# Thresholded attention with a gated mix: q's left-over blocks placed by DMA, the sums' 1e-9 on VectorE, low parts in two pieces, and new planned durations

## The chip, the cores and the metric

The kernel runs on one core of a Trainium2 chip. The metric is the device time of one execution in microseconds. Five engines have queues of their own, each worked off in order: TensorE (PE; its weight loads are PEld in the profile), VectorE (DVE), ScalarE (ACT), GpSimd (POOL) and SyncE (SP), which here only issues DMAs.

## What is computed

```python
# attention: q, k, v are (8 batches, 8 heads, 576 rows, 64)
scores = scale * np.matmul(q, k.transpose(0, 1, 3, 2))
thresh = np.max(scores, axis=-1, keepdims=True) - tau
scores = np.where(scores >= thresh, scores, -1000000000.0)
attn = np.exp(scores - np.max(scores, axis=-1, keepdims=True))
attn = attn / (np.sum(attn, axis=-1, keepdims=True) + 1e-09)
x = attn @ v          # heads side by side: (8, 576, 512)
# gated mix
gate = sigmoid(causal convolution of x over 5 rows, per column, with conv_w)
out = (gate * (x @ w_val)) @ w_out
```

The weights `w_val`, `w_out` and `conv_w` arrive as 64-bit floats.

## The kernel before

Two heads of 64 make a pair that fills the 128 partitions. A **job** is one pair of one batch: 32 jobs (4 pairs x 8 batches). The 576 rows of q are four blocks of 128 and a left-over block of 64; the left-over blocks of both heads make one tile together ("both"), so a job has nine tiles: `both`, and four for each head. Arithmetic is float32: for scores and products every operand is split into a high part (rounded to fp32r by ScalarE, `CAST`) and a low part (the difference, `tensor_sub` on GpSimd), and two or three matmuls add up.

For each job `prepare` fetches k and q (`k_r`, `q_r`, one buffer each), scales q on GpSimd (L327), makes `kh`, `kl`, `qh`, `ql` (L312, L316, L320, L324) and copies them by DMA into `KH`, `KL` and `Q`, where every head lies twice over the partitions (L362, L381). The left-over blocks of q go into a block-diagonal operand `bdq`, on GpSimd (`place`, L338 to L349, through `spread`, L210): four instructions of 64x64 for a job. The first job is loaded straight into place on two queues.

For each tile TensorE makes the scores `s` (L482, two buffers), VectorE takes the row maxima (L486), ScalarE the exponentials and the threshold (L492, L494), and VectorE keeps what is over the threshold and sums it (L508). For each group of two tiles (or the single `both` tile), `turned` adds 1e-9 to the sums on GpSimd (L525), takes the reciprocal on VectorE (L527), divides on whichever of GpSimd, ScalarE or VectorE the planner takes (L538, L534, L536), and turns the block with TensorE (L588) and a ScalarE copy (L599). For each half of a job (320 and 256 rows) `attended` multiplies with v (L627, L634). `convolve` makes high and low parts of the result (L667, L671) and the convolution: tap 0 on GpSimd (L676), four taps on VectorE (L683), the gate on ScalarE. When the four pairs of a batch are done, `products` does x @ w_val (L725), the gating on VectorE (L752), high and low parts (L768, L772), and the product with w_out (L725), which ScalarE takes out and SP sends (L797).

The weights are turned from 64-bit words in 16 units of 128x256 (`Words`, `from_f64`): five VectorE steps (L224 to L233), an addition (L236) and a low part (L268) on GpSimd, and two ScalarE steps.

No order is written by hand. Every step is an `op` with an engine, a due number (in tiles), a planned cost, a planned time until its result is there, and the buffers that it takes and gives. `carry_out` (L140) walks planned time: on each engine it takes the earliest that can begin, of equals the one due first, and emits it. GpSimd and those VectorE steps marked `DVEp` also share one planned `port`: no two of them overlap in the plan. The emitted order on every engine is fixed; on the chip each instruction waits by semaphores for what it really needs. A planned duration therefore only decides the order.

## Time and profile before

| | us |
|---|---|
| median of 3 runs | 774.73 |
| lowest, highest | 774.28, 776.41 |
| span of the profiled execution | 776.5 |
| busy PE / DVE / ACT / POOL in it | 719.6 / 644.3 / 647.2 / 475.7 |

The profiled execution's own time is its span, 776.5 us from the first to the last instruction; it is 1.8 us over the median and lies at the upper end of the runs. Busy time is a mean over stages that have different limits, so the views by stretch, by group and along the chain of waits are read beside it. A matmul's end is modelled and overlaps the next one's start.

### The profile page before, as it was taken

How to read it: one execution, taken by the hardware profiler on the slowest of the kernel's cores; microseconds unless marked ns; L12 is line 12 of the kernel's file. 1: busy time of each engine (PE TensorE's matmuls, PEld its weight loads, DVE VectorE, ACT ScalarE, POOL GpSimd, SP SyncE). 2: the span in 40 equal slices, each digit the busy share in tenths (PEclk: the TensorE clock that was granted, in tenths of full speed). 3: DMA queues.
4: the chain of work that ended last, by engine and by line, in shares of the span. 5: the costliest groups of instructions: out<-in, count | busy, mean ns of one | idle time of the engine just before them, and what ended most of it. 6: DMA issues, size and time to landing. Idle time of an engine off the chain costs nothing.

```text
span 776.5 us, 15682 instructions
## 1 busy us (share of the span) xinstructions
PE 719.6 (93%) x5216; PEld 607.0 (78%) x5216; DVE 644.3 (83%) x1359; ACT 647.2 (83%) x1477; POOL 475.7 (61%) x698
## 2 busy tenths in 40 slices
PE   3788778979999999999999999998999999999997
PEld 3556457867878888888888888887888888978897
DVE  5989998988888887999878887887888888899830
ACT  5898978978998889899889988897898989888832
POOL 4777655847676775677557675765556764745321
PEclk9999989999999999999999999999999999999999
DMA  6666553535464555555465565553555556540001
GB/s 183 172 170 153 151 149 86 151 91 151 124 156 118 125 148 146 141 135 138 111 164 118 129 152 142 143 131 79 152 151 123 126 136 163 144 98 26 32 31 62
DMA packets 51888, 99.03 MB, mean 128 GB/s; under 512 B 9056, under 2 KB 9056, under 8 KB 51808
## 3 DMA queue, kind: packets, MB, share of 16 engines
q1 hardware_dynamic: 51488, 97.47, 49.0%
q8 instruction: 42, 0.69, 0.4%
q10 hardware_dynamic: 320, 0.56, 0.3%
q14 instruction: 38, 0.31, 0.1%
HBM read 35.74 MB, written 9.44 MB: 58 GB/s over the span
## 4 chain that ended last, share of the span: by engine, by line
PE 68%; DVE 15%; DMA 5%; POOL 4%; ACT 4%; issue 2%; SPq 0%; POOLq 0%; ACTq 0%
PE acc L725 20%; PE s L482 17%; PE acc L634 14%; PE tp L588 13%; DVE nm L486 4%; DVE pp L508 4%; PE acc L627 3%; DMA q_r<-qT 3%; DVE pre L683 3%; ACT e L492 1%; POOL pp L538 1%; DVE spare L229 1%; DVE spare_m L231 1%; POOL ql L324 1%; DVE pp L536 1%
## 5 line engine op out<-in xcount | busy, mean ns | idle before, releaser
L486 DVE TENSOR_REDUCE nm<-s 128x1 f32<-128x576 f32 x288 | 214.9, 752 | 46.9 <-PE s L482 43.6
L492 ACT ACTIVATE e<-s,nm 128x576 f32<-128x576 f32 x288 | 215.3, 747 | 29.9 <-DVE nm L486 16.3
L508 DVE SCALAR_TENSOR_TENSOR pp<-s,nm,e 128x576 f32<-128x576 f32 x256 | 206.8, 811 | 19.9 <-ACT nm L494 18.3
L599 ACT COPY T<-tp 128x384 f32<-128x384 f32 x384 | 175.2, 488 | 26.3 <-PE tp L588 24.8
L482 PE MATMUL s<-KH,Q 128*128 128x288 f32 x512 | 163.4, 334 | 34.2 <-DVE pp L508 23.1
L588 PE MATMUL tp<-ident,pp 128*128 128x128 f32 x1152 | 183.3, 280 | 10.8 <-ACT pp L534 3.6
L588 PEld LDWEIGHTS tp<-ident,pp 128*128 128x128 f32 x1152 | 141.2, 143 | 20.9 <-ACT T L599 5.2
L482 PE MATMUL s<-KL,Q 128*128 128x288 f32 x512 | 147.0, 301 | 0.0
L482 PEld LDWEIGHTS s<-KH,Q 128*128 128x128 f32 x512 | 99.9, 195 | 59.6 <-DVE pp L508 32.2
L634 PE MATMUL acc<-T,v 128*64 128x256 f32 (+1 forms) x1024 | 141.2, 419 | 0.0
L538 POOL TENSOR_SCALAR pp<-pp,sums 128x576 f32<-128x576 f32 x124 | 106.9, 867 | 36.1 <-DVE sums L527 32.2
L683 DVE SCALAR_TENSOR_TENSOR pre<-xT,cw,pre 128x576 f32<-128x576 f32 x128 | 118.6, 926 | 8.8 <-POOL pre L676 8.7
L634 PEld LDWEIGHTS acc<-T,v 128*64 128x64 f32 x1024 | 69.1, 139 | 64.9 <-issue 28.0
L482 PEld LDWEIGHTS s<-KL,Q 128*128 128x128 f32 x512 | 99.9, 195 | 0.0
L525 POOL TENSOR_SCALAR sums<-sums 128x2 f32<-128x2 f32 (+1 forms) x160 | 46.9, 293 | 82.5 <-DVE pp L508 66.1
L494 ACT ACTIVATE nm<-nm,less 128x1 f32<-128x1 f32 x288 | 84.8, 294 | 0.0
L725 PE MATMUL acc<-xl,wvh 128*128 128x320 f32 (+1 forms) x256 | 78.3, 306 | 1.0 <-POOL xl L671 1.0
L725 PE MATMUL acc<-xh,wvl 128*128 128x320 f32 (+1 forms) x256 | 79.2, 309 | 0.0
L725 PE MATMUL acc<-gl,woh 128*128 128x320 f32 (+1 forms) x256 | 78.2, 305 | 1.1 <-POOL gl L772 1.1
L725 PE MATMUL acc<-xh,wvh 128*128 128x320 f32 (+1 forms) x256 | 78.6, 307 | 0.1
L725 PE MATMUL acc<-gh,wol 128*128 128x320 f32 (+1 forms) x256 | 78.6, 307 | 0.0
L725 PE MATMUL acc<-gh,woh 128*128 128x320 f32 (+1 forms) x256 | 78.4, 306 | 0.0
(81 smaller groups left out, 1279.8 us busy)
## 6 DMA issues: line engine op xcount, KB each, us to landing
KH<-kh SPq DMA_DIRECT2D x124, 144.0 KB, 2.6
KL<-kl SPq DMA_DIRECT2D x124, 144.0 KB, 3.5
k_r<-kT SPq DMA_DIRECT2D x32, 320.0 KB, 3.8
v<-vs SPq DMA_DIRECT2D x32, 320.0 KB, 2.9
q_r<-qT SPq DMA_DIRECT2D x32, 288.0 KB, 3.9
outT<-o SPq DMA_DIRECT2D x32, 288.0 KB, 2.4
Q<-qh SPq DMA_DIRECT2D x62, 128.0 KB, 2.3
Q<-ql SPq DMA_DIRECT2D x62, 128.0 KB, 2.4
```

The source lines that it names most:

```text
L482: nc.tensor.matmul(s[:, a, :HS], w, m, start=i == 0, stop=i == len(terms) - 1)
L486: nc.vector.tensor_reduce(self.nm[:, 0:1], self.s[:, :, :HS], axis=AX.XY, op=ALU.max, negate=True)
L492: nc.scalar.activation(self.e, self.s[:, :, :HS], AF.Exp, bias=self.nm[:, 0:1])
L494: nc.scalar.activation(self.nm[:, 1:2], self.nm[:, 0:1], AF.Identity, bias=less, scale=-1.0)
L508: nc.vector.scalar_tensor_tensor(grp.p[:, i * S : (i + 1) * S].rearrange("p (a f) -> p a f", a=2), self.s[:, :, :HS], self.nm[:, 1:2], self.e,
L525: add = op("POOL", k - 4, 0.2, 0.33, lambda: nc.gpsimd.tensor_scalar(sums(), sums(), 1.0, 1e-9, op0=ALU.mult, op1=ALU.add), [self.kept])
L538: nc.gpsimd.tensor_scalar(v, v, ri(i), 0.0, op0=ALU.mult, op1=ALU.add)
L588: nc.tensor.transpose(tp[:, i * P : (i + 1) * P], self.p[:, k0 : k0 + P], ident)
L599: nc.scalar.copy(T[:, c0 : c0 + n, self.off : self.off + P], tp[:, 0 : n * P].rearrange("p (c q) -> p c q", q=P),)
L634: nc.tensor.matmul(acc[hs, :w], t.v[:, c0 : c0 + D], T[:, h * NKC + c, :], start=False, stop=c == NKC - 1, skip_group_check=True,)
L683: nc.vector.scalar_tensor_tensor(cv, t.xT[:, i : i + S], cw[:, g, i : i + 1], cv, op0=ALU.mult, op1=ALU.add)
L725: nc.tensor.matmul(taken[name, e, j][:, :w], wt[:, c, c0 : c0 + P], moving(c, i)[:, hs], start=n == 0, stop=n == NM - 1,)
```

## The change

- The left-over blocks of q are copied into `bdq` by four DMAs on SP's queue for each job, in two ops of two, in place of the four GpSimd instructions; each moves 64 rows of 64 numbers.
- 1e-9 is added to the sums by VectorE, in front of the reciprocal, in place of GpSimd: 160 instructions.
- Every low part of k, q, x and g is made in two GpSimd instructions in place of one: 320 and 320 columns for k, 320 and 256 for the others. In the plan, a product of a half then waits for that half's low part alone.
- Planned durations: an SP issue 0.56 us (before 0.1, or 0.15 for a pair), a pair 1.12 us; landing times up to 3.6 us; GpSimd, ScalarE and tap durations by formulas in the number of columns; division 0.66 us on ScalarE (before 0.6) and 0.43 on VectorE (before 0.375); `attended` 0.08 us more; the first job's steps less.
- Without effect on what is emitted: `Pair`, `units` and `js` make it possible to plan a half by itself, which is not used; two switches that were not in use are gone; the PSUM buffers are declared in another order.

```diff
-            add = op("POOL", k - 4, 0.2, 0.33, lambda: nc.gpsimd.tensor_scalar(
-                sums(), sums(), 1.0, 1e-9, op0=ALU.mult, op1=ALU.add), [self.kept])
+            add = op("DVE", k - 4.9, 0.08, 0.2, lambda: nc.vector.tensor_scalar(
+                sums(), sums(), 1e-9, None, op0=ALU.add), [self.kept])
...
-            others = {"DVEp": (0.375, 0.47), "ACT": (0.6, 0.72)}
+            others = {"DVEp": (0.43, 0.52), "ACT": (0.66, 0.78)}
...
                     for hs in HEADS:
                         src = (self.ql if which else self.qh)
-                        spread(self.bd[hs, which, hs], src[hs, 0:SL].bitcast(F32))
+                        nc.sync.dma_start(
+                            self.bd[hs, which, hs].bitcast(F32), src[hs, 0:SL].bitcast(F32)
+                        )
...
-            self.blocks = [op("POOL", due + 3, 0.45, 0.6, place(0), [high], [r_bd])]
-            self.blocks.append(op("POOL", due + 3, 0.45, 0.6, place(1), [low, self.blocks[0]]))
+            self.blocks = []
+            if 0 in self.js:
+                self.blocks = [op("SP", due + 3, 2 * SEND, 2.9, place(0), [high], [r_bd])]
+                self.blocks.append(op("SP", due + 3, 2 * SEND, 2.9, place(1), [low, self.blocks[0]]))
...
+    SEND = 0.56
+    def act(n):
+        return 0.1 + 0.00083 * n
+    def pool1(n):
+        return 0.13 + 0.00102 * n
+    def pool2(n):
+        return 0.17 + 0.00212 * n
+    def tapped(n):
+        return 0.068 + 0.00114 * n
...
-            got_k = op("SP", due - 6, 0.1, 3.8, fetch_k, takes=[r_kr])
+            got_k = op("SP", due - 6, SEND, 3.9, fetch_k, takes=[r_kr])
...
-            self.low_k = op("POOL", due + 1, 1.52, 1.62, low_k, [self.high_k], [r_kl],
-                            [(r_kr, lambda: self.k_r)])
+            self.low_k = [self.high_k]
+            for x in (0, SK // 2):
+                self.low_k = [op(
+                    "POOL", due + 1, pool2(SK // 2), pool2(SK // 2) + 0.1, low_k(x, x + SK // 2),
+                    self.low_k, [] if x else [r_kl], [(r_kr, lambda: self.k_r)] if x else [],
+                )]
...
-                o = op("SP", due + 1, 0.15, 2.9, copies(name, rooms, src, 0), [done], [rooms])
+                o = op("SP", due + 1, 2 * SEND, 3.6, copies(name, rooms, src, 0), done, [rooms])
...
-            cost = 5 * w / 600 + 0.19
+            cost = 5 * w / 600 + 0.27
...
+        lows, done = [], [first]
+        for j in js:
+            c = HALVES[j]
+            m = c.stop - c.start
+            done = [op("POOL", k + 1, pool2(m), pool2(m) + 0.1, low(c), done, [] if j else [r_xl])]
```

Over the whole program the numbers of instructions change so: GpSimd loses 160 additions and 128 placings and gains 128 low parts; VectorE gains the 160 additions; SP gains 128 DMA issues. The divisions move a little: GpSimd 143 to 135, ScalarE 94 to 102, VectorE 51 both times.

**VectorE, the stretch around 80 us** (about the 31st tile; `spare` and `wvh`/`woh` belong to the weights' conversion, `pre` to the taps, `sums` to the groups). Before:

```order
L527 RECIPROCAL sums_137<-sums_137 128x2
L226 SCALAR_TENSOR_TENSOR spare_168<-o_166,spare_m 128x256
L683 SCALAR_TENSOR_TENSOR pre_154<-xT_141,cw_172,pre_154 128x576
L229 SCALAR_TENSOR_TENSOR spare_168<-wvh,spare_168 128x256
L508 SCALAR_TENSOR_TENSOR pp_131,sums_134<-s_101,nm_125,e_123 128x576
L486 TENSOR_REDUCE nm_126<-s_102 128x1
L527 RECIPROCAL sums_133<-sums_133 128x1
L231 TENSOR_SCALAR spare_m<-spare_168 128x256
L683 SCALAR_TENSOR_TENSOR pre_154<-xT_141,cw_172,pre_154 128x576
L233 SCALAR_TENSOR_TENSOR wvh<-o_166,spare_m 128x256
L508 SCALAR_TENSOR_TENSOR pp_131,sums_134<-s_102,nm_126,e_124 128x576
```

The changed kernel at the same tiles:

```order
L534 TENSOR_REDUCE nm_126<-s_106 128x1
L550 SCALAR_TENSOR_TENSOR pp_131,sums_134<-s_105,nm_125,e_123 128x576
L237 TENSOR_SCALAR spare_m<-o_166 128x256
L737 SCALAR_TENSOR_TENSOR pre_154<-xT_141,cw_172,pre_154 128x576
L239 SCALAR_TENSOR_TENSOR spare_168<-o_166,spare_m 128x256
L550 SCALAR_TENSOR_TENSOR pp_131,sums_134<-s_106,nm_126,e_124 128x576
L534 TENSOR_REDUCE nm_127<-s_105 128x1
L567 TENSOR_SCALAR sums_134<-sums_134 128x2
L569 RECIPROCAL sums_134<-sums_134 128x2
```

The addition (L567) stands after the group's second L550, here directly ahead of its reciprocal (L569), as in 94 of the 160 groups; in the other 66 something stands between. The weights' conversion is about one unit further on here; its last unit ends at the same tile, give or take one.

**GpSimd in the steady part, around 515 us** (`kl`, `ql`, `gl` and `xl` are low parts, `pp` and `pl` the blocks to divide, `q_r` the q to scale). Before:

```order
L316 TENSOR_TENSOR kl_110<-k_r_107,kh_109 128x640
L538 TENSOR_SCALAR pp_131<-pp_131,sums_137 128x576
L525 TENSOR_SCALAR sums_133<-sums_133 128x1
L324 TENSOR_TENSOR ql_112<-q_r_108,qh_111 128x576
L210 TENSOR_SCALAR bdq_121<-qh_111 64x64 x2
L210 TENSOR_SCALAR bdq_121<-ql_112 64x64 x2
L538 TENSOR_SCALAR pl_132<-pl_132,sums_133 128x576
L772 TENSOR_TENSOR gl_164<-g_156,gh_160 128x576
L210 TENSOR_SCALAR pl_132<-pl_132 128x64
L525 TENSOR_SCALAR sums_134<-sums_134 128x2
L327 TENSOR_SCALAR q_r_108<-q_r_108,sc 128x576
L538 TENSOR_SCALAR pp_129<-pp_129,sums_134 128x576
```

The changed kernel at the same job:

```order
L342 TENSOR_TENSOR kl_110<-k_r_107,kh_109 128x320
L580 TENSOR_SCALAR pp_130<-pp_130,sums_136 128x576
L342 TENSOR_TENSOR kl_110<-k_r_107,kh_109 128x320
L836 TENSOR_TENSOR gl_164<-g_156,gh_160 128x320
L836 TENSOR_TENSOR gl_164<-g_156,gh_160 128x256
L580 TENSOR_SCALAR pl_132<-pl_132,sums_133 128x576
L223 TENSOR_SCALAR pl_132<-pl_132 128x64
L356 TENSOR_TENSOR ql_112<-q_r_108,qh_111 128x320
L356 TENSOR_TENSOR ql_112<-q_r_108,qh_111 128x256
L580 TENSOR_SCALAR pp_129<-pp_129,sums_134 128x576
L364 TENSOR_SCALAR q_r_108<-q_r_108,sc 128x576
L580 TENSOR_SCALAR pp_130<-pp_130,sums_135 128x576
```

The four `bdq` instructions and the additions are gone from between the others, a division stands between the two pieces of `kl`, and two divisions now stand ahead of the scaling of q_r and right behind it.

**SP at the second and third job** (`bdq` are the left-over blocks, `KH`, `KL`, `Q` the copied parts). Before:

```order
L362 DMA KH_118<-kh_109 64x576 x2
L362 DMA KL_120<-kl_110 64x576 x2
L304 DMA k_r_107<-kT 128x640
L362 DMA KH_118<-kh_109 64x576 x2
L381 DMA Q_116<-qh_111 64x512 x2
L362 DMA KL_120<-kl_110 64x576 x2
L308 DMA q_r_108<-qT 128x576
L381 DMA Q_116<-ql_112 64x512 x2
```

The changed kernel:

```order
L392 DMA bdq_121<-qh_111 64x64 x2
L328 DMA k_r_107<-kT 128x640
L332 DMA q_r_108<-qT 128x576
L392 DMA bdq_121<-ql_112 64x64 x2
L435 DMA Q_116<-qh_111 64x512 x2
L414 DMA KH_118<-kh_109 64x576 x2
L392 DMA bdq_122<-qh_111 64x64 x2
L414 DMA KL_120<-kl_110 64x576 x2
L328 DMA k_r_107<-kT 128x640
L264 DMA o_166<-w_val 128x512
L414 DMA KH_118<-kh_109 64x576 x2
L332 DMA q_r_108<-qT 128x576
```

Two pairs of issues for each job came in: the one of the high part ahead of the copies of `KL` and of the next fetch of k, the one of the low part behind the next fetch of q. On TensorE the second job's `both` scores, ahead of the first half's products with v before, now stand behind them.

## Rows read from the trace of the kernel before

**Rows 1.** Busy time by stretch: us, then the busy us (and instructions) of PE, PEld, DVE, ACT and POOL, the granted clock as a share of full speed, the mean busy share of the DMA engines and GB/s. The first row is the stretch in which the weights are turned from 64-bit words, the second the steady part, the third the end.
```profile
20.00:180.00 160.00, 129.78 (x826) 99.40 (x826) 145.50 (x318) 133.81 (x309) 108.26 (x162) 0.93 0.53 138
180.00:745.00 565.00, 554.66 (x4165) 474.16 (x4162) 480.05 (x1004) 494.58 (x1134) 352.31 (x510) 1.00 0.50 127
745.00:776.50 31.50, 26.89 (x202) 26.24 (x200) 7.88 (x12) 7.31 (x15) 7.14 (x6) 0.97 0.12 48
```

**Rows 2.** The chain of waits of the stretch from 20 to 180 us, summed by line (shares of the stretch).
```profile
by line: PE s L482 13.2%; PE acc L634 11.4%; DVE nm L486 10.7%; DVE pp L508 8.0%; PE tp L588 6.6%; DVE spare L229 4.7%; issue 4.6%; PE acc L725 4.1%; DVE pre L683 4.1%; ACT e L492 3.9%; DVE spare_m L231 3.8%; PE acc L627 3.3%; DVE spare L22
```

**Rows 3.** GpSimd's groups over the whole run (page, part 5, and the groups by shape): line, engine, operation, output<-input, shapes, count | busy us, mean ns of one | idle us before them and what ended it. The first is both shapes of the 1e-9 add, the next two the placing of q's left-over blocks, the last four the low parts.
```profile
L525 POOL TENSOR_SCALAR sums<-sums 128x2 f32<-128x2 f32 (+1 forms) x160 | 46.9, 293 | 82.5 <-DVE pp L508 66.1
L210 POOL TENSOR_SCALAR bdq<-qh 64x64 fp32r<-64x64 f32 x64 | 17.2, 268 | 3.1
L210 POOL TENSOR_SCALAR bdq<-ql 64x64 fp32r<-64x64 f32 x64 | 16.6, 259 | 3.8
L316 POOL TENSOR_TENSOR kl<-k_r,kh 128x640 fp32r<-128x640 f32 x32 | 51.2, 1600 | 14.3 <-ACT kh L312 13.3
L324 POOL TENSOR_TENSOR ql<-q_r,qh 128x576 fp32r<-128x576 f32 x32 | 46.5, 1454 | 13.7 <-ACT qh L320 11.8 <-POOL sums L525 0.7
L671 POOL TENSOR_TENSOR xl<-xT,xh 128x576 fp32r<-128x576 f32 x32 | 47.6, 1487 | 4.2 <-ACT xh L667 3.9
L772 POOL TENSOR_TENSOR gl<-g,gh 128x576 fp32r<-128x576 f32 x32 | 46.8, 1464 | 19.9 <-ACT gh L768 19.3
```

**Rows 4.** VectorE's groups from 20 to 180 us, same columns: the row maxima, three steps of the weights' conversion, and the reciprocals of pairs and of single sums.
```profile
L486 DVE TENSOR_REDUCE nm<-s 128x1 f32<-128x576 f32 x58 | 43.2, 751 | 11.8 <-PE s L482 11.3
L231 DVE TENSOR_SCALAR spare_m<-spare 128x256 int32<-128x256 int32 x16 | 10.1, 633 | 0.0
L226 DVE SCALAR_TENSOR_TENSOR spare<-o,spare_m 128x256 int32<-128x256 int32 x16 | 9.2, 574 | 0.0
L229 DVE SCALAR_TENSOR_TENSOR spare<-woh,spare 128x256 f32<-128x256 f32 x8 | 8.3, 1039 | 0.0
L527 DVE RECIPROCAL sums<-sums 128x2 f32<-128x2 f32 x26 | 4.0, 153 | 0.0
L527 DVE RECIPROCAL sums<-sums 128x1 f32<-128x1 f32 x7 | 1.1, 152 | 0.0
```

**Rows 5.** The same three conversion steps over the whole run, one line of code each: count, then shortest/median/longest ns of one.
```profile
L231 DVE TENSOR_SCALAR spare_m<-spare x16: 276/310/1632, 28.4 to 178.5; 128x256 int32<-128x256 int32 x16
L226 DVE SCALAR_TENSOR_TENSOR spare<-o,spare_m x16: 404/426/1765, 20.3 to 175.8; 128x256 int32<-128x256 int32 x16
L229 DVE SCALAR_TENSOR_TENSOR spare<-woh,spare x8: 414/1122/1637, 100.9 to 177.4; 128x256 f32<-128x256 f32 x8
```

**Rows 6.** The timeline of GpSimd (POOL) and VectorE (DVE) at two places: start us, us, engine, line, operation, output<-input, shapes, count.
```profile
15.83 0.75 POOL L538 TENSOR_SCALAR pp<-pp,sums 128x576 f32<-128x576 f32 x1
...
16.26 0.34 DVE L226 SCALAR_TENSOR_TENSOR cw<-cw_raw,cw 128x20 int32<-128x20 int32 x1
17.26 0.17 DVE L229 SCALAR_TENSOR_TENSOR cw<-cw,cw 128x20 f32<-128x20 f32 x1
17.47 0.18 DVE L231 TENSOR_SCALAR cw<-cw 128x20 int32<-128x20 int32 x1
...
80.78 1.59 POOL L316 TENSOR_TENSOR kl<-k_r,kh 128x640 fp32r<-128x640 f32 x1
...
80.48 0.15 DVE L527 RECIPROCAL sums<-sums 128x2 f32<-128x2 f32 x1
80.55 0.41 DVE L226 SCALAR_TENSOR_TENSOR spare<-o,spare_m 128x256 int32<-128x256 int32 x1
80.89 2.09 DVE L683 SCALAR_TENSOR_TENSOR pre<-xT,cw,pre 128x576 f32<-128x576 f32 x1
```

**Rows 7.** Who waited for whom over the whole run: engine and line, what ended the wait: us in total, times, longest us.
```profile
POOL q_r L327 <- DMA q_r<-qT: 35.6, 14, 8.8
```

**Rows 8.** Pieces of the chain of waits around 520 us, in order of time: start us, us, what.
```profile
518.26 0.24 POOL bdq L210
...
519.25 4.54 DMA q_r<-qT
...
524.63 0.73 POOL pp L538
...
525.87 2.62 DVE pp L536 x2
```

**Rows 9.** SyncE's queue: one pair of DMA issues in the timeline (start us, us), and from the DMA issues by tile the median us from issue to landing of the pieces of q that are nearest in size to the new ones.
```profile
447.77 1.10 SPq L362 DMA_DIRECT2D KH<-kh  x2
...
Q<-qh SPq DMA_DIRECT2D x62, 128.0 KB, 2.3
```

**Rows 10.** The timeline where the last piece of a pair's left-over blocks is placed (POOL, bdq<-ql) and where TensorE first uses them (PE, s<-kh,bdq): the second pair, and one of the steady part.
```profile
28.80 0.56 POOL L210 TENSOR_SCALAR bdq<-ql 64x64 fp32r<-64x64 f32 x2
...
29.64 0.53 PE L482 MATMUL s<-kh,bdq 128*128 128x288 f32 x2 [0.24 <-DVE pp L508]
...
500.36 0.54 POOL L210 TENSOR_SCALAR bdq<-ql 64x64 fp32r<-64x64 f32 x2
...
535.88 0.43 PE L482 MATMUL s<-kh,bdq 128*128 128x288 f32 x2
```

**Rows 11.** TensorE's timeline where the last products wait at the end.
```profile
761.51 0.42 PE L725 MATMUL acc<-gl,woh 128*128 128x320 f32 x1 [1.06 <-POOL gl L772]
```

More of the change, by code (lines that the diff above doesn't have):

```diff
@@ L19 @@
 P = 128
-AHEAD = False
-TH = "ACT"
 DIVIDE = ("DVEp", "ACT")
@@ L728, in run @@
                         )
[L730 to L732 removed]
+                    after = [*need[c][j][i], weights[name, c, c0 // CW * CW], *last]
                     cost = 0.147 if j == 0 else 0.118
```

283 lines of the change are left out of this document (163 added, 120 removed).

## The prediction

> **What bounds the kernel now.** Read first the busy time by stretch [rows 1]. In the steady part, from 180 to 745 us, TensorE is busy 554.7 of 565 us, so at most 10.3 us are to be had there; VectorE has 85 us free, ScalarE 70. Before it, from 20 to 180 us, TensorE works only 129.8 of 160 us (30.2 idle, at a granted clock of 0.93), while VectorE is busy for 145.5. There the products have no input yet and VectorE carries the weights' conversion beside the tiles. The chain of that stretch [rows 2] goes to and fro between the two: VectorE's maxima, L508, taps and conversion on one side, scores, products with v and transposes on the other. At the end TensorE is alone, with one wait for GpSimd [rows 1, 11].
>
> Second, VectorE's own time in that early stretch is not all work. Three conversion steps take 633, 574 and 1039 ns on average [rows 4] and 276, 404 and 414 ns at the shortest [rows 5]: 16 x 0.357 + 16 x 0.170 + 8 x 0.625 = 13.4 us more than their work. What they wait for is seen in the timeline: a tap that began at 80.89 us, 0.11 us after a low part of 1.59 us on GpSimd, took 2.09 us [rows 6]. VectorE stands still while a GpSimd instruction that began before it runs.
>
> **The change, part by part.** The sums are made against the profiled execution's 776.5 us; the median of the runs is 1.8 lower, and I take the 1.8 off at the end.
>
> *GpSimd's time.* It loses the additions (46.9 us) and the placings (17.2 + 16.6) [rows 3] and gains 128 instructions for the split. Two widths give a line: 1600 ns at 640 columns and about 1468 at 576 make 2.06 ns a column and 0.28 us fixed, so the split costs at most 128 x 0.28 = 36 us. GpSimd ends at least 45 us lighter. It is busy 352 of 565 us in the steady part [rows 1], so this is nothing by itself; it counts through the waits of VectorE and through what queues on it.
>
> *VectorE's waits in the early stretch.* The four groups of low parts are 192 of GpSimd's some 470 us [rows 1, 3], two fifths, and about twice as long as the others, so I put half of the waits down to them; a piece half as long leaves half the wait: 13.4 x 0.5 x 0.5 = 3.4 us. The additions and placings are many but short (0.26 to 0.29 us): I give them a twentieth, 0.7. Together -4.1. The bounds are 0 (the planner only moves the overlaps) and -8 (the low parts' whole half, with some of the taps).
>
> *The additions on VectorE.* Nothing shows an addition of two numbers there. The nearest rows are small steps that follow one another: 0.07 us from a reciprocal to the next instruction when that needs nothing of it, 0.21 us from one small `cw` step to the next that needs it [rows 6]. 94 of the 160 additions stand directly ahead of their reciprocal; I take 0.21 for those and 0.07 for 66, 24 us in all, 0.15 each. In the early stretch, 33 groups [rows 4] cost 33 x 0.15 = +5.0 us (2.3 to 6.9), and there it lies on the path. In the steady part 19 us go into VectorE's 85 free ones; I put +1 for the times when TensorE waits for scores' buffers. If that cover is gone, all 19 count.
>
> *The place around 520 us.* There the chain runs through a placing, then a fetch of q (4.54 us), a division that stands on GpSimd behind the scaling of that q, and two divisions on VectorE that take 2.62 us because a low part is under way [rows 8]. GpSimd stood waiting for q 14 times, 35.6 us in all [rows 7], with divisions queued behind. The changed order has one division ahead of the scaling at this place and no placings. TensorE has only 10.3 us idle in the steady part, so I take -2 (0 to -6).
>
> *Left-over blocks by DMA.* A pair of issues takes SP 1.10 us, and a piece lands 2.3 us after issue [rows 9]; against 0.56 us on GpSimd that is some 2.8 us later. In the steady part the blocks lie ready 35 us (500.9 to 535.9) before TensorE uses them: hidden. For the second job they are ready 0.3 us before, at 29.36 for 29.64 [rows 10]; there and for the first job it can show: 0 to 2 x 2.8 = +5.6. The second job's `both` scores now stand behind the products with v, which covers most of it; I take +1.5. SP's 2.2 us more for a job lie in a job's time of more than 20 us.
>
> *The end.* The last products wait 1.06 us for the last low part of g [rows 11]. With two pieces the first product needs only the first, some 0.6 us earlier. -0.6, and -0.5 for 13 products fewer behind the last product with v (between 0 and 13 x 0.13).
>
> *The planned durations.* The plan counted 0.15 us for a pair of issues that takes 1.10 [rows 9], and too little for divisions and products with v. What a truer order is worth no row shows; the nearest is that in the early stretch VectorE waited 11.3 us for scores before the maxima [rows 4], in a stretch in which TensorE was idle for 30.2. A plan that fits would remove some of this mutual waiting. I take -5, under half of the 11.3; the bounds are -20, two thirds of TensorE's idle time there, and +10, as much the other way, since every order changes.
>
> Sum: -4.1 + 5.0 + 1 - 2 + 1.5 - 0.6 - 0.5 - 5 = -4.7, so 771.8 in the profiled execution and 770.0 as a median: 0.6% faster. What this measurement can tell from no change is about 0.3%, 2.3 us.
>
> **The rivals.**
>
> *The new order fits much better.* The early stretch loses two thirds of its idle time: 15 us below the forecast, 755. For it: 30.2 us of idle TensorE in 160 [rows 1], an SP plan that was wrong by a factor of seven, GpSimd's waits for q [rows 7]. Against it: the early stretch is full on VectorE as well, 145.5 of 160, which new durations do not empty.
>
> *The order is worth nothing.* Without the -5 the sum is 0.3, the median 775: no change. For it: the steady part is at TensorE's bound, and relief and additions on VectorE cancel in the early stretch (-4.1 + 5.0).
>
> *The additions wait for GpSimd* (slower). A step of 20 columns (L226, `cw`) took 344 ns while a division was under way on GpSimd, and the next small step 0.17 us [rows 6]; so small instructions on VectorE can be held as well. The plan counts the addition as free of this. The reciprocal is not held: 153 and 152 ns on average [rows 4], on the same data. Price, if the addition is held: GpSimd is busy about half of the time, the instruction under way is then some 0.75 us long and half of it is left, less the little that the addition takes anyway: 0.5 x 0.32 = 0.16 us for each, 160 x 0.16 = 26 us on VectorE. In the early stretch 33 x 0.16 = 5.3 count in full; in the steady part VectorE comes to (480 + 19 + 20) / 565 = 92% and TensorE must begin to wait, for which I count a third of the 20, 7. That is 12 above the forecast, 782. It decides from a wait of some 0.07 us for each addition, where the gain of 4.7 is used up. The Trainium skill has a rule that speaks for this rival ("SBUF — State Buffer", "Who interferes with whom"): `tensor_scalar` is among the operations that can enter a 2-port mode, and then it and a GpSimd instruction shut each other out, the later one waiting for the whole of the other. The trace agrees for the conversion's `tensor_scalar` (L231, 276 to 1632 ns, [rows 5]); no run here shows it for one or two columns, and by that rule the time would be this rival's 782.
>
> *The order fits worse*, by the +10 of the bound and no gain: 785. It is the same unknown as the first rival with the other sign, and the longer waits for the left-over blocks (+5.6) would be part of it.
>
> **How the numbers follow.** The forecast, 764 to 772.4, has 0.36; the better order, 745 to 764, has 0.22; no change, 772.4 to 777, has 0.18; the held additions 0.15, and a worse order 0.09. Faster by over 0.3% is therefore 0.36 + 0.22 = 0.58, within it 0.18, slower 0.24. The range for 8 in 10 goes from 752 to 784: about 0.08 of the better order lies below it, and 0.12 of the slower cases above. I predict 770.
>
> **What would show it.** Right: the early stretch's VectorE loses most of the excess of L231, L226 and L229; the new additions take about 0.15 us with no wait on GpSimd; TensorE is idle for less than 30 us between 20 and 180 us and about 10 in the steady part; GpSimd is 45 us or more lighter. Wrong: additions with a mean well above 0.15 us and a wide spread (the third rival); TensorE waiting for `bdq` at the first two jobs; idle time of TensorE in the steady part well over 10 us, with VectorE's L508 or SP's landings named; or an early stretch that is shorter by 15 us or more, which would mean that I gave the order too little.

## The result and the profile after

| | before | after |
|---|---|---|
| median of 7 runs each on one chip, us | 775.18 | 780.69 |
| lowest to highest | 774.12 to 780.47 | 778.45 to 782.51 |
| ratio, 95% interval | | 1.0057 (1.003 to 1.0084) |
| span of the profiled execution | 776.5 | 780.7 |

The change makes the kernel 0.57% slower, with an interval that lies wholly above 1; 770.0 was predicted, 0.6% faster.

Busy time by stretch of the changed kernel, same columns as [rows 1]:

```profile
20.00:180.00 160.00, 130.38 (x839) 98.87 (x840) 146.19 (x341) 133.49 (x305) 101.10 (x129) 0.96 0.55 143
180.00:745.00 565.00, 554.94 (x4125) 469.25 (x4123) 512.99 (x1138) 498.35 (x1141) 298.52 (x374) 1.00 0.51 129
745.00:780.70 35.70, 31.61 (x232) 29.37 (x230) 7.94 (x12) 9.55 (x20) 9.58 (x11) 1.00 0.12 45
```

And over its whole span (page, part 1):

```profile
PE 724.3 (93%) x5216; PEld 603.0 (77%) x5216; DVE 678.6 (87%) x1519; ACT 652.6 (84%) x1485; POOL 416.1 (53%) x530
```

GpSimd is 59.6 us lighter and VectorE 34.3 us fuller, 33 of these in the steady part. TensorE's busy time tells nothing here: it is idle for 10.1 of the 565 us, before for 10.3, but 4125 matmuls fall into that stretch and not 4165. A matmul's end is modelled, so a slower stream of matmuls still reads as busy; the count beside the time is the measure. At 134 ns (554.94 us by 4125) the 40 missing matmuls are 5.4 us. Further places are told by two marks of TensorE's trace, the first product with v of the seventh job and that of the last half. Before:

```profile
184.18 0.70 PE L627 MATMUL acc<-T,v 128*128 128x320 f32 x2
...
741.30 0.61 PE L627 MATMUL acc<-T,v 128*128 128x256 f32 x2
```

After:

```profile
184.27 0.74 PE L670 MATMUL acc<-T,v 128*128 128x320 f32 x2
...
747.07 0.59 PE L670 MATMUL acc<-T,v 128*128 128x256 f32 x2
```

The 4.2 us of the two spans are +0.1 up to the first mark, +5.7 between the marks and -1.6 behind the second.

The chain that ended last (page, part 4), before, by engine:

```profile
PE 68%; DVE 15%; DMA 5%; POOL 4%; ACT 4%; issue 2%; SPq 0%; POOLq 0%; ACTq 0%
```

After, by engine and by line:

```profile
PE 54%; DVE 28%; ACT 8%; DMA 4%; issue 3%; SPq 1%; POOL 1%; POOLq 0%; ACTq 0%; DVEq 0%
PE acc L788 16%; PE s L530 14%; PE acc L677 11%; PE tp L630 10%; DVE pp L550 8%; DVE nm L534 7%; DVE pre L737 7%; PE acc L670 3%; ACT e L540 3%; DMA q_r<-qT 2%; DVE sums L567 2%; ACT T L641 1%; DVE pl L550 1%; ACT nm L541 1%; DVE g L812 1%
```

VectorE's share of the chain was 15% and is 28% now, and the additions (L567) are in it themselves. Their groups and those of the reciprocals behind them, by shape:

```profile
L567 DVE TENSOR_SCALAR sums<-sums 128x2 f32<-128x2 f32 x128 | 39.5, 308 | 0.8
L569 DVE RECIPROCAL sums<-sums 128x2 f32<-128x2 f32 x128 | 20.6, 161 | 2.7
L567 DVE TENSOR_SCALAR sums<-sums 128x1 f32<-128x1 f32 x32 | 4.5, 142 | 0.2
```

Both by line of code (count, shortest/median/longest ns):

```profile
L567 DVE TENSOR_SCALAR sums<-sums x160: 125/160/875, 15.5 to 741.0; 128x2 f32<-128x2 f32 x128, 128x1 f32<-128x1 f32 x32
...
L569 DVE RECIPROCAL sums<-sums x160: 136/165/168, 15.7 to 741.2; 128x2 f32<-128x2 f32 x128, 128x1 f32<-128x1 f32 x32
```

An addition of two columns takes 308 ns on average and up to 875; the reciprocal of the same two columns never takes over 168. Sorted by whether a GpSimd instruction was under way at its start and for 60 ns more, the 128 additions of two columns fall apart: 498 ns on average for 56 with one, 160 (150 to 172) for 72 without. Of the 56, 55 end 21 to 31 ns after the GpSimd instruction that they met; together they wait 56 x 0.34 = 19 us. The 32 of one column take 144 and 139. One of the long ones in the timeline of the changed kernel (start us, us, engine, line):

```profile
429.96 1.69 POOL L342 TENSOR_TENSOR kl<-k_r,kh 128x320 fp32r<-128x320 f32 x2 [1.60 <-ACT kh L336]
...
430.77 0.15 DVE L569 RECIPROCAL sums<-sums 128x2 f32<-128x2 f32 x1
430.85 0.83 DVE L567 TENSOR_SCALAR sums<-sums 128x2 f32<-128x2 f32 x1
...
431.71 0.17 DVE L569 RECIPROCAL sums<-sums 128x2 f32<-128x2 f32 x1
431.76 0.19 PEld L530 LDWEIGHTS s<-KH,Q 128*128 128x128 f32 x1 [0.49 <-DVE sums L567]
```

The second piece of a `kl` is under way until 431.65; the addition of 430.85 ends at 431.68, and a reciprocal runs past in 0.15 us just before it. The weight load of the next scores is shown as waiting 0.49 us for the addition, but that is no lost time: the scores begin 0.36 us after the start of the last product with v, and at all 42 places of this kernel where scores follow such products that is 0.31 to 0.36 us.

The relief that was forecast is there. First the taps' group in the kernel before, which [rows 4, 5] do not hold:

```profile
L683 DVE SCALAR_TENSOR_TENSOR pre<-xT,cw,pre 128x576 f32<-128x576 f32 x128 | 118.6, 926 | 8.8 <-POOL pre L676 8.7
```

In the changed kernel, the groups of the conversion steps of [rows 5] (L239, L244, L242 now) and of the taps:

```profile
L239 DVE SCALAR_TENSOR_TENSOR spare<-o,spare_m 128x256 int32<-128x256 int32 x16 | 8.3, 517 | 0.0
L244 DVE TENSOR_SCALAR spare_m<-spare 128x256 int32<-128x256 int32 x16 | 5.7, 354 | 0.1
L242 DVE SCALAR_TENSOR_TENSOR spare<-woh,spare 128x256 f32<-128x256 f32 x8 | 4.8, 594 | 0.0
L737 DVE SCALAR_TENSOR_TENSOR pre<-xT,cw,pre 128x576 f32<-128x576 f32 x128 | 125.3, 979 | 10.8 <-POOL pre L730 10.8
```

GpSimd's low parts, which answer to the last four of [rows 3], and its wait of [rows 7]:

```profile
L342 POOL TENSOR_TENSOR kl<-k_r,kh 128x320 fp32r<-128x320 f32 x64 | 58.8, 925 | 45.4 <-ACT kh L336 43.7
L356 POOL TENSOR_TENSOR ql<-q_r,qh 128x320 fp32r<-128x320 f32 x64 | 53.4, 842 | 24.9 <-ACT qh L350 23.0 <-DMA Q<-ql 1.8
L721 POOL TENSOR_TENSOR xl<-xT,xh 128x320 fp32r<-128x320 f32 x64 | 56.0, 891 | 8.6 <-ACT xh L715 8.6
L836 POOL TENSOR_TENSOR gl<-g,gh 128x320 fp32r<-128x320 f32 x64 | 55.9, 890 | 24.6 <-ACT gh L829 24.4
```

```profile
POOL q_r L364 <- DMA q_r<-qT: 40.2, 13, 5.4
```

Measured against the shortest rows of [rows 5], the three steps wait for 16 x 0.078 + 16 x 0.113 + 8 x 0.180 = 4.5 us and not 13.4. But 128 taps now take 53 ns more each, 6.7 us: a part of the waits has moved to other VectorE steps. The splitting costs GpSimd 224.1 - 192.1 = 32 us, within the 36 that were allowed for it.

### The profile page after: what moved, and what is told of

Its sections match the earlier page's. It is cut to its first block, busy times and chain, and to the rows that moved or that the text cites. A ratio compares the mean times of both kernels' runs of the same rounds, so it can differ in the third digit from the quotient of the medians.

```text
span 780.7 us, 15997 instructions
## 1 busy us (share of the span) xinstructions
PE 724.3 (93%) x5216; PEld 603.0 (77%) x5216; DVE 678.6 (87%) x1519; ACT 652.6 (84%) x1485; POOL 416.1 (53%) x530
## 4 chain that ended last, share of the span: by engine, by line
PE 54%; DVE 28%; ACT 8%; DMA 4%; issue 3%; SPq 1%; POOL 1%; POOLq 0%; ACTq 0%; DVEq 0%
PE acc L788 16%; PE s L530 14%; PE acc L677 11%; PE tp L630 10%; DVE pp L550 8%; DVE nm L534 7%; DVE pre L737 7%; PE acc L670 3%; ACT e L540 3%; DMA q_r<-qT 2%; DVE sums L567 2%; ACT T L641 1%; DVE pl L550 1%; ACT nm L541 1%; DVE g L812 1%
## 5 line engine op out<-in xcount | busy, mean ns | idle before, releaser
L550 DVE SCALAR_TENSOR_TENSOR pp<-s,nm,e 128x576 f32<-128x576 f32 x256 | 206.4, 811 | 20.9 <-ACT nm L541 15.8
L641 ACT COPY T<-tp 128x384 f32<-128x384 f32 x384 | 175.1, 486 | 20.0 <-PE tp L630 19.1
L630 PEld LDWEIGHTS tp<-ident,pp 128*128 128x128 f32 x1152 | 137.8, 142 | 29.6 <-ACT T L641 11.9
L530 PE MATMUL s<-KL,Q 128*128 128x288 f32 x512 | 145.2, 298 | 0.0
L580 POOL TENSOR_SCALAR pp<-pp,sums 128x576 f32<-128x576 f32 x118 | 96.7, 825 | 76.5 <-DVE sums L569 47.1
L737 DVE SCALAR_TENSOR_TENSOR pre<-xT,cw,pre 128x576 f32<-128x576 f32 x128 | 125.3, 979 | 10.8 <-POOL pre L730 10.8
L342 POOL TENSOR_TENSOR kl<-k_r,kh 128x320 fp32r<-128x320 f32 x64 | 58.8, 925 | 45.4 <-ACT kh L336 43.7
```

Of the source, the lines that this page charges most:

```text
L342: nc.gpsimd.tensor_sub(self.kl[:, x:y], self.k_r[:, x:y], self.kh[:, x:y].bitcast(F32))
L530: nc.tensor.matmul(s[:, a, :HS], w, m, start=i == 0, stop=i == len(terms) - 1)
L550: nc.vector.scalar_tensor_tensor(grp.p[:, i * S : (i + 1) * S].rearrange("p (a f) -> p a f", a=2), self.s[:, :, :HS], self.nm[:, 1:2], self.e,
L580: nc.gpsimd.tensor_scalar(v, v, ri(i), 0.0, op0=ALU.mult, op1=ALU.add)
L630: nc.tensor.transpose(tp[:, i * P : (i + 1) * P], self.p[:, k0 : k0 + P], ident)
L641: nc.scalar.copy(T[:, c0 : c0 + n, self.off : self.off + P], tp[:, 0 : n * P].rearrange("p (c q) -> p c q", q=P),)
```

## The experiments

Each ratio is to the kernel before on the same chip, with its 95% interval. "Marks" are the two of TensorE's trace from above.

| run | ratio | span, us | first mark | between the marks |
|---|---|---|---|---|
| before | 1 | 776.5 | 184.2 | 557.1 |
| after | 1.0057 (1.0030 to 1.0084) | 780.7 | 184.3 | 562.8 |
| e1_no_add | 0.9899 (0.9873 to 0.9926) | 770.9 | 181.7 | 555.6 |
| e5_two_single_adds | 0.9947 (0.9924 to 0.9970) | 774.0 | 181.4 | 559.0 |
| e14_one_sum_of_three_operands | 1.0101 (1.0076 to 1.0126) | 780.2 | 183.6 | 562.9 |
| e2_add_gpsimd | 1.0127 (1.0100 to 1.0155) | 782.5 | 182.6 | 566.2 |
| e3_add_only | 1.0351 (1.0315 to 1.0387) | 804.9 | 192.7 | 577.8 |
| e13_before_two_single | 1.0263 (1.0226 to 1.0300) | 797.9 | 191.9 | 571.5 |
| e9_old_durations | 1.0114 (1.0092 to 1.0137) | 783.3 | 195.7 | 554.0 |
| e12_two_single_old | 1.0065 (1.0037 to 1.0094) | 777.3 | 194.1 | 549.6 |
| e4_durations_only | 1.0132 (1.0099 to 1.0165) | 784.1 | 196.4 | 551.5 |
| e10_sp_durations_only | 0.9996 (0.9976 to 1.0016) | 774.0 | 184.6 | 554.5 |
| e11_other_durations | 1.0086 (1.0056 to 1.0116) | 783.6 | 186.1 | 562.3 |
| e8_bd_split | 1.0053 (1.0029 to 1.0076) | 778.4 | 180.3 | 564.5 |
| e16_two_single_sp_old | 0.9869 (0.9844 to 0.9893) | 767.7 | 181.6 | 552.5 |
| e17_two_single_rest_old | 0.9986 (0.9967 to 1.0005) | 777.1 | 185.0 | 558.5 |

### Is it the additions, and is it their waiting?

**e1_no_add**, the changed kernel in its own order with the 160 additions of 1e-9 left out:

```diff
-            add = op("DVE", k - 4.9, 0.08, 0.2, lambda: nc.vector.tensor_scalar(
-                sums(), sums(), 1e-9, None, op0=ALU.add), [self.kept])
+            add = op("DVE", k - 4.9, 0.08, 0.2, lambda: None, [self.kept])
```

> The changed kernel with the 160 additions of 1e-9 left out (the plan still counts them, so every other instruction stands in the same order). Theory A (the additions of two columns are held by GpSimd and fill VectorE): the 56 held ones alone took 56 x 0.34 = 19 us of VectorE, all 160 some 44 us; without them about 770 to 774. Theory B (the new order is worse by itself, the additions lie in VectorE's free time): 779 to 782, as the changed kernel.

**e5_two_single_adds**, the additions as two of one column each:

```diff
-            add = op("DVE", k - 4.9, 0.08, 0.2, lambda: nc.vector.tensor_scalar(
-                sums(), sums(), 1e-9, None, op0=ALU.add), [self.kept])
+            def plus():
+                for i in range(n):
+                    x = self.sums[:, i : i + 1]
+                    nc.vector.tensor_scalar(x, x, 1e-9, None, op0=ALU.add)
+            add = op("DVE", k - 4.9, 0.08, 0.2, plus, [self.kept])
```

> The changed kernel, same order, with the addition of two columns made as two additions of one column each. In the changed kernel's trace the 32 additions of one column took 0.14 us whether GpSimd was at work or not, those of two 0.50 with it and 0.16 without. Theory A: no addition is held any more, 128 more instructions of 0.07 to 0.14 us come in (9 to 18 us) against 19 us of waits: 776 to 781, mean of an addition about 0.14 us. Theory B: 779 to 783. If they are held after all: 0.3 us each and over 783.

**e14_one_sum_of_three_operands**, one instruction over the same columns that is not `tensor_scalar`:

```diff
-            add = op("DVE", k - 4.9, 0.08, 0.2, lambda: nc.vector.tensor_scalar(
-                sums(), sums(), 1e-9, None, op0=ALU.add), [self.kept])
+            add = op("DVE", k - 4.9, 0.08, 0.2, lambda: nc.vector.scalar_tensor_tensor(
+                sums(), sums(), 1e-9, sums(), op0=ALU.add, op1=ALU.max), [self.kept])
```

> The changed kernel in its own order, with the addition written as scalar_tensor_tensor, the larger of (sums + 1e-9) and sums, over the same two columns in one instruction; the numbers are the same. It tells whether the hold belongs to tensor_scalar or to the width. If only tensor_scalar of two columns is held: 145 to 200 ns whatever GpSimd does, and the time of the run with two single additions or a little less, 770 to 775, ratio 0.993 to 0.999. If scalar_tensor_tensor from SBUF is held as well (as the taps are, 789 to 1511 ns): additions of two columns near 500 ns with a GpSimd instruction under way, and the changed kernel's time, 778 to 782, ratio 1.003 to 1.008.

**e2_add_gpsimd**, the addition issued on GpSimd at the place that the plan has for VectorE's:

```diff
-            add = op("DVE", k - 4.9, 0.08, 0.2, lambda: nc.vector.tensor_scalar(
-                sums(), sums(), 1e-9, None, op0=ALU.add), [self.kept])
+            add = op("DVE", k - 4.9, 0.08, 0.2, lambda: nc.gpsimd.tensor_scalar(
+                sums(), sums(), 1.0, 1e-9, op0=ALU.mult, op1=ALU.add), [self.kept])
```

> The changed kernel, same order and plan, but the addition is issued on GpSimd as before, at its place in time. Theory A: VectorE is rid of the additions, the reciprocal waits for GpSimd again: 772 to 777. Theory B: 779 to 783.

The additions in e5 and e14, and the reciprocal in e2:

```profile
L570 DVE TENSOR_SCALAR sums<-sums 128x1 f32<-128x1 f32 x288 | 31.8, 144 | 0.2
```

```profile
L567 DVE SCALAR_TENSOR_TENSOR sums<-sums 128x2 f32<-128x2 f32 x128 | 38.3, 299 | 0.8
L567 DVE SCALAR_TENSOR_TENSOR sums<-sums 128x1 f32<-128x1 f32 x32 | 11.9, 373 | 0.2
```

```profile
L569 DVE RECIPROCAL sums<-sums 128x2 f32<-128x2 f32 (+1 forms) x160 | 25.5, 160 | 46.4 <-POOL sums L567 45.2
```

Without the additions the change is a gain of 1.0%; with additions that are not held, of 0.5%; with held ones a loss of 0.6%. By these ratios and the 775.18 us of the kernel before, e1 stands at 767 and e5 at 771, both lower than the theory of the waits expected (770 to 774, 776 to 781) and away from its rival's 779 to 783. In e5 288 instructions take 143 ns each where a GpSimd instruction is under way and 145 where none is, and the two of a group overlap, so that a group costs 0.20 us (31.8 by 160) against 0.27 in the changed kernel (43.7 by 160). The 19 us of waiting are gone, the second instructions take some of that back, and VectorE's additions are 12 us shorter in all, 0.074 for each. These 12 us cost 1.0057 - 0.9947 = 1.1%, 8.5 us. The order of the instructions is the same on every engine but for the second addition, so this is shown to be the waiting. VectorE's share of the chain falls with it, from 28% to 22% (16% in e1).

TensorE's matmuls can therefore be compared one by one. Of the 3.8 us by which the changed kernel is slower than e5 between the marks, 2.1 lie ahead of scores, 1.8 of these where they wait for VectorE's L550, and 1.8 ahead of transposes, 1.3 of these where they wait for ScalarE's copies (L641). No wait of a matmul that is over 0.1 us long is ended by an addition, so the cost comes through the steps that stand behind the additions and begin later.

In e14 the held form is another (488 ns on average for two columns with a GpSimd instruction under way, 153 without): it costs what the changed kernel costs or somewhat more, 1.0101 where 1.003 to 1.008 was expected of a held form. Leaving the engine (e2) does not help in this order, because the reciprocal then waits for GpSimd 45 us in all; my expectation for it, 772 to 777, named that wait and priced it too low, and at 785 by the ratio it is above the rival's 779 to 783 as well.

### The same addition in other orders

**e3_add_only**, the kernel before with only the addition moved (low parts whole):

```diff
-            add = op("POOL", k - 4, 0.2, 0.33, lambda: nc.gpsimd.tensor_scalar(
-                sums(), sums(), 1.0, 1e-9, op0=ALU.mult, op1=ALU.add), [self.kept])
+            add = op("DVE", k - 4.9, 0.08, 0.2, lambda: nc.vector.tensor_scalar(
+                sums(), sums(), 1e-9, None, op0=ALU.add), [self.kept])
```

> The kernel before with only the addition moved to VectorE. Theory A: its additions of two columns are held as in the changed kernel, and longer, since the low parts are whole (up to 1.4 us): mean 0.3 to 0.4 us; 780 to 790. Theory C: the addition costs little, 774 to 778.

**e13_before_two_single**, e3 with two additions of one column:

```diff
-            add = op("DVE", k - 4.9, 0.08, 0.2, lambda: nc.vector.tensor_scalar(
-                sums(), sums(), 1e-9, None, op0=ALU.add), [self.kept])
+            add = op("DVE", k - 4.9, 0.08, 0.2, plus, [self.kept])
```

> The kernel before, with the addition of 1e-9 on VectorE as in the changed kernel, but as two additions of one column each where the group has two; nothing else changed. It is the run with the addition alone (ratio 1.0351 to before) without what holds it. Theory A (a two-column addition waits for the GpSimd instruction under way, a one-column addition does not): one-column additions near 145 ns, with or without a GpSimd instruction under way; VectorE carries 288 x 0.145 = 42 us instead of 51, without long waits ahead of the reciprocal; the time falls back to 775 to 783, ratio 1.000 to 1.010. Rival (in this order the addition costs as a wait of its own on VectorE, or the order after it is a bad one, whatever its duration): 795 or more, ratio above 1.025.

**e9_old_durations**, the changed kernel with the planned durations of the kernel before for SP, the divisions, `attended`, the exponential and the first job (the formulas by number of columns stay, here and in e12, e16, e17 and e8):

```diff
-            got_k = op("SP", due - 6, SEND, 3.9, fetch_k, takes=[r_kr])
+            got_k = op("SP", due - 6, 0.1, 3.8, fetch_k, takes=[r_kr])
...
-            others = {"DVEp": (0.43, 0.52), "ACT": (0.66, 0.78)}
+            others = {"DVEp": (0.375, 0.47), "ACT": (0.6, 0.72)}
...
-            cost = 5 * w / 600 + 0.27
+            cost = 5 * w / 600 + 0.19
```

> The changed kernel with the planned durations of before for SP, divisions, products with v, exponentials and the first job (all three other parts stay, the addition of two columns on VectorE too). Theory A (held additions are the loss, the order is a draw of its own): slower than before by about as much as the changed kernel, 778 to 785, with a mean addition of two columns near 0.3 us. Theory C (the new durations cost some 1.3%, as the run with them alone, and the other parts give part of it back): 768 to 775.

**e12_two_single_old**, e9 with two additions of one column:

```diff
-            add = op("DVE", k - 4.9, 0.08, 0.2, lambda: nc.vector.tensor_scalar(
-                sums(), sums(), 1e-9, None, op0=ALU.add), [self.kept])
+            add = op("DVE", k - 4.9, 0.08, 0.2, plus, [self.kept])
```

> The changed kernel with the planned durations of the kernel before (as in the run that gave 1.0114), and the addition as two of one column. It is a third order in which the hold alone is taken away. Theory A: the time falls by about as much as in the changed kernel (1.0057 to 0.9947), to 774 to 779, ratio 0.999 to 1.005, and the loss of some 10 us at 180 to 200 us stays in part, as it belongs to the order. Rival (the held additions cost only where the planned durations are new): 783 or more, ratio 1.010 or above.

The additions of e3:

```profile
L525 DVE TENSOR_SCALAR sums<-sums 128x2 f32<-128x2 f32 x128 | 46.8, 365 | 0.8
L525 DVE TENSOR_SCALAR sums<-sums 128x1 f32<-128x1 f32 x32 | 4.7, 146 | 0.3
```

With whole low parts a held addition takes 766 ns on average and up to 1529, against 498 and 875 with halves. At 802 by the ratio e3 lies above the 780 to 790 that its theory gave. Taking the wait away gains in all three orders: 1.0351 to 1.0263, 1.0114 to 1.0065 (between theory and rival, nearer to the theory), 1.0057 to 0.9947. But e13 stays at 1.0263, above the 1.000 to 1.010 of my theory and above the rival's bound of 1.025: in this order the larger part of the loss is not the wait. What is left is the order and the additions' own time, which no run here separates. One place of the order is seen. TensorE's stretch from 180 to 200 us, in e13 and in e12 (columns as in [rows 1]):

```profile
180.00:200.00 20.00, 15.05 (x71) 10.10 (x70) 15.38 (x41) 13.63 (x31) 11.35 (x17) 0.74 0.54 145
```

```profile
180.00:200.00 20.00, 14.74 (x76) 9.18 (x76) 14.73 (x39) 13.10 (x29) 12.20 (x17) 0.74 0.58 152
```

In the kernel before and the changed kernel 149 and 152 matmuls fall into these 20 us, here 71 and 76; e3 (66), e9 (70) and e4 (54) have the same gap; at 134 ns for each missing matmul it is worth 10 to 13 us. In e13 that is about half of the 21 us by which its span is longer: it is 8.4 us behind the kernel before at the 1200th matmul and 18.7 at the 3200th. The rest is lost in the steady part and was not traced. At the granted clock of 0.74 a part of it is run at the lower level, 1.2 GHz, after TensorE has stood. It is where the first batch's product with w_out meets the last units of the weights' conversion. In these five orders ScalarE takes out the first rows of `o` behind 65 to 70 exponentials, and VectorE's last step of `woh` stands behind 68 to 71 row maxima; in the eleven kernels without the gap (before and after among them) those are 58 to 61 and 59 to 64. So the planner either gets the conversion done before these tiles or has it run into them. That the late place causes the gap is read from this list and from the waits there, not shown by moving that place alone.

### What the planned durations are worth

**e4_durations_only**, the kernel before with all planned durations of the changed kernel and nothing else:

```diff
-            got_k = op("SP", due - 6, 0.1, 3.8, fetch_k, takes=[r_kr])
+            got_k = op("SP", due - 6, SEND, 3.9, fetch_k, takes=[r_kr])
...
-            others = {"DVEp": (0.375, 0.47), "ACT": (0.6, 0.72)}
+            others = {"DVEp": (0.43, 0.52), "ACT": (0.66, 0.78)}
```

> The kernel before with only the planned durations of the change (SP issues 0.56, divisions 0.66 and 0.43, products with v 0.08 more, formulas for the rest); the instructions are those of before, in another order. Theory A: the order is not the cause, so at or below before, 765 to 776. Theory B: the whole loss, 779 to 783.

**e10_sp_durations_only**, of these only SP's:

```diff
-                o = op("SP", due + 1, 0.15, 2.9, copies(name, rooms, src, 0), [done], [rooms])
+                o = op("SP", due + 1, 1.12, 3.6, copies(name, rooms, src, 0), [done], [rooms])
```

> The kernel before with only SP's planned durations new. If the loss of the run with all new durations (ratio 1.013) is SP's part: 785 to 792, and a stretch like the one at 180 to 200 us there, where TensorE lost 13 us. If that was one unlucky place of one order: no such stretch, 772 to 780.

**e11_other_durations**, only those of the first job, exponential, divisions and `attended`:

```diff
-            others = {"DVEp": (0.375, 0.47), "ACT": (0.6, 0.72)}
+            others = {"DVEp": (0.43, 0.52), "ACT": (0.66, 0.78)}
...
-            cost = 5 * w / 600 + 0.19
+            cost = 5 * w / 600 + 0.27
```

> The kernel before with new planned durations for the first job's steps, the exponential, the divisions and the products with v alone (SyncE's and the preparation's as before). All durations together gave 1.0132, with TensorE losing 13 us at 180 to 200 us; SyncE's alone 0.9996 with no loss there. If these durations (0.05 us more for a division, 0.08 more for the products with v) bring that loss: 783 to 792, ratio 1.010 to 1.020, with the loss at 180 to 200 us again. If it takes both together, or those of the preparation: 773 to 778, ratio 0.997 to 1.003.

**e16_two_single_sp_old** and **e17_two_single_rest_old**, e5 with SP's durations set back, and with the others set back:

```diff
-                o = op("SP", due + 1, 2 * SEND, 3.6, copies(name, rooms, src, 0), done, [rooms])
+                o = op("SP", due + 1, 0.15, 2.9, copies(name, rooms, src, 0), done, [rooms])
```

> The changed kernel with two additions of one column, and SyncE's planned durations alone set back to those of the kernel before (0.1 us for an issue, 0.15 for a pair, and the landing times). Both sets new gave 0.9947, both old 1.0065 with TensorE losing 9.8 us at 180 to 200 us and 9 us less behind it. If SyncE's durations hold back the steady part and the others remove the loss at 180 to 200: 763 to 769 where before has 775, ratio 0.985 to 0.992. If SyncE's durations remove the loss: near 780, ratio 1.004 to 1.010. If each order is a case of its own: between, with losses at other places.

```diff
-            others = {"DVEp": (0.43, 0.52), "ACT": (0.66, 0.78)}
+            others = {"DVEp": (0.375, 0.47), "ACT": (0.6, 0.72)}
```

> The changed kernel with two additions of one column, and the planned durations of the first job, the exponential, the divisions and the products with v set back, SyncE's new. If the loss at 180 to 200 us belongs to these durations it is there again: near 780, ratio 1.004 to 1.010, or more where SyncE's new durations hold back the steady part as well (785, 1.013). If SyncE's durations remove the loss and these hold back the steady part: 763 to 769, ratio 0.985 to 0.992.

**e8_bd_split**, the kernel before with the placing by DMA and the low parts in two pieces, the addition on GpSimd and the old durations (as a diff to the changed kernel):

```diff
-            others = {"DVEp": (0.43, 0.52), "ACT": (0.66, 0.78)}
+            others = {"DVEp": (0.375, 0.47), "ACT": (0.6, 0.72)}
...
-            add = op("DVE", k - 4.9, 0.08, 0.2, lambda: nc.vector.tensor_scalar(
-                sums(), sums(), 1e-9, None, op0=ALU.add), [self.kept])
+            add = op("POOL", k - 4, 0.2, 0.33, lambda: nc.gpsimd.tensor_scalar(
+                sums(), sums(), 1.0, 1e-9, op0=ALU.mult, op1=ALU.add), [self.kept])
```

> The kernel before with the left-over blocks by DMA and the split low parts, the addition on GpSimd and the old durations. If the blocks by DMA show at the first two jobs, TensorE's first products with v come 2 us later or more than before (30.5 us). If the relief of GpSimd is worth something (some 4 us on VectorE in the early stretch): 768 to 776. If every new order costs: 778 to 790.

In the kernel before, SP's new durations are worth nothing (0.9996) and the others lose 0.9% (e11: neither of its expectations, the loss is there but not the gap). Together, and with the formulas by number of columns, which neither of the two has, they bring the gap and lose 1.3% (e4: 785 by the ratio, above both of its expectations); what the formulas do by themselves was not tried. In the changed kernel SP's and the others gain: 1.0114 to 1.0057 with held additions, 1.0065 to 0.9947 without. The four runs with single additions take that apart. Old durations of both kinds: the gap, first mark at 194.1, then the shortest way between the marks, 549.6. Either kind new: no gap, first mark at 181.6 or 185.0, so that e17 fits neither of its two expectations: in this kernel the gap needs both kinds old. SP's new: the way between the marks is 558.5 or 559.0; SP's old: 549.6 or 552.5. So SP's "true" durations cost 6.5 to 8.9 us in the steady part of this kernel (in the kernel before, e10, that way is 2.6 us shorter with them), and the best is to leave them as they were: e16, at 0.9869, is 1.3% faster than the kernel before and the fastest of all that keep the additions. Its chain (page, part 4) is TensorE's again:

```profile
PE 68%; DVE 18%; ACT 8%; DMA 3%; issue 2%; POOL 1%; POOLq 0%; SPq 0%; ACTq 0%; DVEq 0%
```

And from 200 to 740 us, by line, for e5 and then e16:

```profile
by line: PE acc L792 18.7%; PE s L530 17.1%; PE acc L681 13.8%; PE tp L634 13.7%; DVE pre L741 6.5%; DVE pp L550 4.9%; DVE nm L534 4.1%; DMA q_r<-qT 3.6%; PE acc L674 3.3%; ACT e L540 2.3%; issue 1.7%; ACT T L645 1.0%; ACT pp L580 0.9%; ACT
```

```profile
by line: PE acc L792 24.7%; PE s L530 20.1%; PE tp L634 17.2%; PE acc L681 16.2%; PE acc L674 3.8%; DVE pre L741 3.2%; DVE pp L550 2.9%; DVE nm L534 2.8%; ACT e L540 1.4%; issue 1.2%; ACT T L645 1.0%; DMA q_r<-qT 0.8%; DVE pl L550 0.7%; ACT
```

The fetch of q all but leaves the chain (3.6% of 540 us is 19 us, 0.8% is 4), and the shares of the taps and the row maxima fall by a half and by a third. GpSimd waits for q no less (55.6 us in e16, 45.1 in e5), so it is where the wait falls that counts. Which SP step does it was not tried one by one. e8 says that placing and splitting (with the formulas by number of columns), in their own order, lose 0.5%: 779 by the ratio, in the 778 to 790 expected if every new order costs.

## Why the prediction was wrong

**The step that failed** is "The additions on VectorE": "I take 0.21 for those and 0.07 for 66, 24 us in all, 0.15 each". They took 43.7 us, 0.27 each, because 56 of the 128 with two columns waited 0.34 us on average until a GpSimd instruction was over. The term was put at +6; leaving the additions out (e1) shows 1.0057 - 0.9899 = 1.6%, 12.2 us. The third rival, "The additions wait for GpSimd", is what happened, at 780.69 where it gave 782. It decides, in its own words, from "a wait of some 0.07 us for each addition"; the wait was 0.12 (19 us by 160), under the 0.16 that it took. Its price was too low for its wait: 26 us on VectorE were to cost 12, and the 12 us between e5 and the changed kernel cost 8.5. Of the 6.7 us between the spans of e5 and the changed kernel, 2.9 lie ahead of the first mark, and 3.8 behind it, in the stretch for which I counted only a third. Most of the 3.8 come through scores that wait for L550 and transposes that wait for ScalarE, and not through TensorE waiting for an addition. The sign of a small step's wait was in [rows 6]; I gave this rival a chance of 0.15 and held the sign against the reciprocals of [rows 4], which are another operation and are not held.

The Trainium skill's rule that was cited ("SBUF — State Buffer", "Who interferes with whom") held for two columns as for 256: 498 ns with a GpSimd instruction under way, 160 without. By the same section of the Trainium skill a VectorE instruction with two SBUF inputs contends with a GpSimd instruction that reads SBUF; e14 agrees, with 488 ns and 153. By the Trainium skill ("VectorE: DVE Perf Modes", "Mode 2×_2P") the mode splits the operand in two halves; that one column escapes agrees with this, since there is nothing to split, and the 288 such additions of e5 took at most 156 ns.

**The rest of the sum was right in total, in part by luck.** With additions that are not held (e5) the ratio is 0.9947, 4.1 us under the kernel before; the sum was -4.7. Without any (e1) it is 7.8 us under, where the sum without its +6 gives 10.7. With the old durations and additions that are not held (e12) the change loses 5.0 us, where the sum without its -5 gives +0.3: the durations did more than was set, and the other terms less.

- *Additions without the wait*: 0.20 us and not 0.15; from e1 to e5 they cost 0.48%, 3.7 us, where +6 was set. All of it lies in the steady part, between the marks (555.6 to 559.0), and nothing in the early stretch (181.7 and 181.4): the cover was sought at the wrong place.
- *VectorE's waits in the early stretch*, -4.1: the three steps lose 8.9 us of waiting, and the taps take 6.7 over the whole run. Right in kind; its worth by itself was not isolated.
- *The place around 520 us*, -2: gone. From 515 to 535 us TensorE is busy for 20.00 us with 153 matmuls; before it was 17.10 us and 124. GpSimd's wait for q falls elsewhere (40.2 us in all, more than in [rows 7]). Of the 2.62 us of two divisions in [rows 8] the reading was half right: the first met GpSimd's tap 0 (from 525.76 us, 0.75 long), only the second a low part (from 526.77, 1.40 long).
- *Left-over blocks by DMA*, +1.5: the first job's products with v begin at 30.88 us, before at 30.54. At the second job TensorE stands 0.74 us for `bdq` (at 37.31 us), a sign of being wrong that was named; in e5 it is 2.2 us there, in e9 and e12 3.2 and 3.3. The bounds hold.
- *The end*, -0.6 - 0.5: TensorE's wait for the last low part is 0.52 us (1.06 in [rows 11]), and the stretch behind the second mark is 1.6 us shorter.
- *Planned durations*, -5: in the changed kernel -0.57% (-4.4 us) with held additions, -1.2% (-9.1 us) without. That the size came near was luck: by the marks of e9 and the changed kernel it is the difference of -11.4 us ahead of the first mark (the gap at 180 to 200) and +8.8 between the marks (SP's durations), not less mutual waiting in the early stretch, and in the kernel before all new durations together lose 1.3%.

Of the signs that were named, "TensorE is idle for less than 30 us between 20 and 180 us and about 10 in the steady part" came true (29.6 and 10.1) in a kernel that is slower. Idle time was the wrong sign; the marks were the right one, and in the steady part the count of matmuls (from 20 to 180 us it rose by 13, and the first mark did not move).

The parts do not add up: addition alone +3.5%, durations alone +1.3%, placing and splitting +0.5%, all together +0.6%. Each part changes the order of everything, and one gap of 10 to 13 us comes and goes with it.

## What to carry to other kernels

A tiny VectorE instruction next to a busy GpSimd is priced by what it may wait for, not by its columns; before it is moved, ask whether its form is one that is held, and whether a form exists that is not (here one column at a time, 1.1% of the kernel). A planned duration in a greedy planner is a knob and not a measurement: the truer numbers for SP made the steady part of the changed kernel 6.5 to 8.9 us longer, so each group of numbers is tried by itself. Where matmul ends are modelled, compare kernels by when the same product begins, or by the number of matmuls, and not by busy time. A wait named on a weight load is not yet lost time: look whether the matmuls begin later than they do elsewhere.

## What was not expected of the hardware

- The same `tensor_scalar` in place takes 498 ns on two columns and 144 on one with a GpSimd instruction under way; without one 160 and 139.
- `scalar_tensor_tensor` with both inputs in SBUF waits even on one column: 373 ns on average against 142 for the `tensor_scalar`.
- The reciprocal of two columns does not wait: 168 ns at the longest of 160.
- A held addition lasts until the GpSimd instruction ends, and 21 to 31 ns more (55 of 56 in the changed kernel, 40 of 43 in e3): 875 ns at most with low parts of 320 columns, 1529 with whole ones.
